# A tuned attention and feed-forward kernel: its program as a list of small steps in a searched order, with loads and stores on other queues and some transposes on TensorE

## Chip, cores and metric

One core of one Trainium2 chip. The metric is the device time of one execution in microseconds (us); lower is better. Single executions of one kernel agree within about 2%. Each time below is a median over runs, most of them "fast" (no run over 1.5% above the fastest of the same kernel); where slow runs matter, the text says so. "SyncE's queue" is the list of DMAs that SyncE issues, in order; "landing" is the time from the issue of a DMA until its data has arrived.

## The reference, cut to what matters

```python
def _attn_ref(q, k, v):                      # 8 batches, 8 heads, 576 tokens, 64 wide
    phi = lambda x: np.where(x > 0, x, np.exp(x) - 1.0) + 1.0
    q_p, k_p = phi(q), phi(k)
    kv = einsum('bhsd,bhse->bhde', k_p, v);  z = sum(k_p, axis=2)
    return einsum('bhsd,bhde->bhse', q_p, kv) / (einsum('bhsd,bhd->bhs', q_p, z)[..., None] + 1e-6)

x = attn.transpose(0, 2, 1, 3).reshape(4608, 512)
out = (((x @ w1) * (x @ w2)) @ w3) @ w_out   # d_ff 1024
```

All inputs and the output are float32 in HBM.

## The kernel before

Per batch it loads q, k and v (1 MB each plus small remainders for tokens 512 to 575), computes phi, forms kv on TensorE, transposes phi(q) into `qt` with a DMA transposition, multiplies (the "numerator units", tile `nd`), divides, and transposes the result `xn` into `xt` with another DMA transposition. The feed-forward part runs on chunks of 512 tokens: the gate (`a_ps`, `b_ps`, then `ab`) and the output (`o_ps`, with w3 and w_out folded into `wf` at the start). A hand-made order interleaves batch n + 1 with chunk n.

The parts that the change touches: who issues which DMA.

```python
def load_qkv(name, src, b, part=None):
    ...
    ins = nc.sync.dma_start(out=t[:, h0 * W:h1 * W]..., in_=src[b, h0:h1, 0:NJ * P, :]...)   # 1 MB
    if part != 1:
        for hh in range(2):                                                                  # remainders
            (nc.sync if part is None else nc.scalar).dma_start(out=t[hh * R:(hh + 1) * R, JW:]..., in_=...)

def qt_load(b, part):                       # part 0: qt, 512 KB; part 1: qtr, the remainder
    ...
    nc.sync.dma_start(out=dst, in_=src, transpose=True)

def xt_load(b, part):
    ...
    nc.sync.dma_start(out=dst, in_=src, transpose=True)

def o_unit(c, m):
    ...                                     # 8 matmuls, a copy to o_sb, then
    nc.gpsimd.dma_start(out=dst[:, j, :], in_=o_sb)
```

So loads and transpositions share SyncE's queue; GpSimd issues weights and stores. The order is text such as this, for the chunks from the fourth on (`L` load, `K`/`Q` phi, `KV`, `N` numerator unit, `X` xt, `T` qt, `V` copies of v, `F` gate, `O` output):

```python
NEXT = """KV F0 Lk Ke0 F1 Ks0 Ks1 O0 N0 Ke1 Ks2 Ks3 KsR F2 N1 O1 Lq N2 F3 N3 X0 Qe0 Qs0 Qs1
          O2 N4 X1 F4 Qe1 Qs2 O3 Lv F5 Qs3 QsR V T F6 F7"""
```

Of the kernel before, what the change touches and what calls it, by code (L numbers as in the profile page):

```python
# [13 lines left out]
P = 128  # L14
# [4 lines left out]
def kernel(  # L19
# [36 lines left out]
    ld = ctx.enter_context(tc.tile_pool(name="ld", bufs=5))  # L56
    setup = ctx.enter_context(tc.tile_pool(name="setup", bufs=2))
# [33 lines left out]
    def load_qkv(name, src, b, part=None):  # L91


        if part is None or part == 0:
            raw[name, b] = ld.tile([P, JW + RW], F32, tag="ld", name=f"{name}32")
        t = raw[name, b]
        h0, h1 = (0, H) if part is None else (4 * part, 4 * part + 4)
        W = NJ * D
        ins = nc.sync.dma_start(
            out=t[:, h0 * W:h1 * W].rearrange("p (h x) -> p h x", x=W),  # L100
            in_=src[b, h0:h1, 0:NJ * P, :].rearrange("h (p j) d -> p h (j d)", j=NJ))
        if part != 1:
            for hh in range(2):
                (nc.sync if part is None else nc.scalar).dma_start(
                    out=t[hh * R:(hh + 1) * R, JW:].rearrange("p (h d) -> p h d", d=D),
                    in_=src[b, hh * 4:(hh + 1) * 4, NJ * P:S, :].rearrange("h p d -> p h d"))
        return ins
# [4 lines left out]
    def phi_steps(name, b):  # L112
        x = raw[name, b]
        e = e_p.tile([P, JW + RW], BF16, tag="e", name="e")
        dj = phi_p.tile([P, KC, NJ, 2, D], BF16, tag=name + "j", name=name + "j")
        dr = phi_p.tile([P, RW], BF16, tag=name + "r", name=name + "r")
        ph[name, b] = (dj, dr)

        def ex(c0, c1):
            nc.scalar.activation(out=e[:, c0:c1], in_=x[:, c0:c1], func=AF.Exp)  # L120
            nc.vector.tensor_scalar_min(out=e[:, c0:c1], in0=e[:, c0:c1], scalar1=1.0)  # L121

        def st(out, ap):
            nc.vector.scalar_tensor_tensor(  # L124
                out=out, in0=ap(x), scalar=1.0, in1=ap(e), op0=ALU.add, op1=ALU.max)

        def pair(hp):
            for u in range(2):
                h = 2 * hp + u
                st(dj[:, hp, :, u, :], lambda t: t[:, h * NJ * D:(h + 1) * NJ * D].rearrange(  # L130
                    "p (j d) -> p j d", d=D))

        return dict(e0=lambda: ex(0, JW // 2), e1=lambda: ex(JW // 2, JW + (RW if b else 0)),
                    eR=lambda: None if b else ex(JW, JW + RW),
                    s0=lambda: pair(0), s1=lambda: pair(1), s2=lambda: pair(2),
                    s3=lambda: pair(3), sR=lambda: st(dr, lambda t: t[:, JW:]))

    def v_unit(b, parts=(0, 1, 2)):
        x = raw["v", b]
        for i in parts:  # L140
            if i < 2:
                nc.scalar.copy(  # L142
                    out=vt[:, :, 4 * i:4 * i + 4, 0:D],
                    in_=x[:, 0:JW].rearrange("p (h j d) -> p j h d", h=H, j=NJ)[
                        :, :, 4 * i:4 * i + 4])
            else:
                nc.scalar.copy(out=vr[:, :, 0:D], in_=x[:, JW:].rearrange("p (h d) -> p h d", d=D))
# [30 lines left out]


    def qt_load(b, part):  # L180
        qj, qr = ph["q", b]
        if part == 0:
            t = att.tile([P, KC, NJ * P], BF16, tag="qt", name="qt")
            src = qj.rearrange("p c j u d -> p (c j u d)")
            dst = t.rearrange("p c (j t) -> p (c j) t", t=P)
        else:
            t = att.tile([P, 2, P], BF16, tag="qtr", name="qtr")
            src, dst = qr, t
        qts[b, part] = t
        nc.sync.dma_start(out=dst, in_=src, transpose=True)  # L190

    def nat_unit(b, j):


        nd = at_ps.tile([P, 2, 512], F32, tag="at", name="nd")
        if j == 0:
            xns[b] = att.tile([P, NJ, H, D], BF16, tag="xn", name="xn")
        if j < NJ:
            n, dst = P, xns[b][:, j]
        else:  # L200
            n = R
            dst = xns[b, "R"] = att.tile([R, H, D], BF16, tag="xnr", name="xnr")
        for hp in range(KC):
            if j < NJ:
                w = qts[b, 0][:, hp, j * P:(j + 1) * P]
            else:
                hh, i = divmod(hp, 2)
                w = qts[b, 1][:, i, hh * R:(hh + 1) * R]
            for u in range(2):
                rows = slice(u * D, (u + 1) * D)  # L210
                nc.tensor.matmul(nd[0:n, u, hp * (D + 1):(hp + 1) * (D + 1)], w[rows],  # L211
                                 kvs[b][rows, hp, u, :], start=True, stop=True)
        v4 = nd[0:n, :, 0:KC * (D + 1)].rearrange("p u (c e) -> p u c e", e=D + 1)
        r = lr.tile([P, 2, KC], F32, tag="r", name="r")
        nc.vector.tensor_scalar_add(out=r[0:n], in0=v4[:, :, :, D], scalar1=1e-6)
        nc.vector.reciprocal(out=r[0:n], in_=r[0:n])
        nc.vector.tensor_tensor(  # L217
            out=dst.rearrange("p (c u) e -> p u c e", u=2), in0=v4[:, :, :, 0:D],
            in1=r[0:n].unsqueeze(3).to_broadcast([n, 2, KC, D]), op=ALU.mult)
# [15 lines left out]
    def first_tr(g):  # L235
# [4 lines left out]
        for i in range(2):  # L240
            for j in range(NJ):
                nc.tensor.transpose(tp[:, i * NJ + j, :],  # L242
                                    qj[:, 2 * g + i, j].rearrange("p u d -> p (u d)"), ident)
        nc.scalar.copy(out=qts[0, 0][:, 2 * g:2 * g + 2, :].rearrange("p i (j t) -> p (i j) t", t=P),
                       in_=tp)

    def first_kv(g):
        kv_half(0, g)
        for n in "zn":
            kvz[n, g] = att.tile([P, 2, 2, D], BF16, tag="kv" + n, name="kv" + n, bufs=2)  # L250
        t = kvs[0][:, 2 * g:2 * g + 2]
# [4 lines left out]
    def first_nd(hp, own):  # L256
# [6 lines left out]
        for i, n in ((1, "z"), (0, "n")):  # L263
            nc.tensor.matmul(nd[i], kvz[n, g][:, a].rearrange("p h e -> p (h e)"),
                             qts[0, 0][:, hp], start=True, stop=True)

        def finish():
            r = lr.tile([P, 512], F32, tag="lr", name="lr", bufs=2)
            nc.scalar.activation(out=r, in_=nd[1], func=AF.Ln, bias=eps[:, 0:1])
            nc.scalar.activation(out=r, in_=r, func=AF.Exp, scale=-1.0)  # L270
            nc.vector.tensor_tensor(
                out=xt[:, 0:NJ, hp, :], in0=nd[0].rearrange("p (j t) -> p j t", t=P),
                in1=r.rearrange("p (j t) -> p j t", t=P), op=ALU.mult)
        return finish
# [25 lines left out]
    def o_unit(c, m):  # L300
# [6 lines left out]
        nc.scalar.copy(out=o_sb, in_=o_ps)  # L307
        kind, b, j = order[c * (NCH // P) + m]
        if kind == "J":
            dst = out[b * S:b * S + NJ * P, :].rearrange("(p j) n -> p j n", j=NJ)  # L310
            nc.gpsimd.dma_start(out=dst[:, j, :], in_=o_sb)  # L311
        else:
            for i in range(2):
                nc.gpsimd.dma_start(
# [21 lines left out]
    def load_w3(i):  # L336
        if i % 4 == 0:
            t = ld.tile([P, JW + RW], F32, tag="ld", name="w3b")
            w3s[i // 4] = t[:, 0:JW].bitcast(BF16).rearrange("p (i n) -> p i n", i=4)
# [6 lines left out]
    def w3_tr(i):  # L346
# [4 lines left out]
        nc.scalar.copy(out=t, in_=tp)  # L351

    def wf_mm(i):
# [4 lines left out]
        nc.scalar.copy(out=wf_sb[:, i, :], in_=ps)  # L358


    def run(steps, names):
        for n in names.split():
            steps[n]()

    ctx.enter_context(tc.manual_schedule())
    src = {"k": k, "q": q, "v": v}

    def load(name, b, part=None):
        return load_qkv(name, src[name], b, part)

    first_loads = [load(n, 0, i) for i in range(2) for n in "kqv"]
    nc.scalar.preload_act_table_set("natural_log_exp_and_others")
    wl = [i for x in range(4) for i in load_w12(x)]
    after(wl[0], first_loads[3])
    wl += [load_wo(0), load_wo(1)]
    wl += [load_w3(i) for i in range(FC)]

    ks, qs = phi_steps("k", 0), phi_steps("q", 0)
    run(ks, "e0 s0 s1 eR sR")
    run(qs, "e0 s0 s1 eR sR")  # L380
    v_unit(0, (0, 2))
    run(ks, "e1 s2 s3")
    run(qs, "e1 s2 s3")
    first_tr(0)
    v_unit(0, (1,))
    first_kv(0)
    first_tr(1)
    fin = [first_nd(0, True), first_nd(1, True)]
    first_kv(1)
    for fn in fin:  # L390
        fn()
    fin = [first_nd(2, False), first_nd(3, False)]
    qt_load(0, 1)
    for fn in fin:
        fn()

    first = [f_open(0, 0), f_open(0, 1)]
    for n, kc in enumerate(range(KC)):
        for f in range(2):
            for ps, w in zip(first[f], (w1_sb, w2_sb)):  # L400
                nc.tensor.matmul(ps, w[:, kc, f * P:(f + 1) * P], xt[:, 0:4, kc, :],
                                 start=(n == 0), stop=(n == KC - 1))
    for f in range(2):
        f_close(0, f, *first[f])
    after(load("q", 1), wl[11])
    load("k", 1)
    load("v", 1)
    for f in range(2, FC):
        f_unit(0, f)
        if f >= 6:  # L410
            w3_tr(f - 6)




    def slots(text, c, a, n, load_b):
        ks = qs = None
        if n < B and n > 0:
            ks, qs = steps[n]
        for u in text.split():  # L420
            if u[0] == "F":
                f_unit(c, int(u[1]))
            elif u[0] == "O":
                o_unit(c - 1, int(u[1]))
            elif u[0] == "W":
# [83 lines left out]
```

## Time and profile before

| | before |
|---|---|
| median time | 278.87 us at first, 278.03 with the later run |
| profiled span | 276.8 us |
| TensorE, VectorE, ScalarE busy | 86%, 57%, 51% |
| mean granted TensorE clock | 0.983 |
| qt transposition, issue to landing (min, median, max) | 3.8, 7.2, 7.8 us |

The page of a profile has three parts that are used here: the busy time of each engine with its share of the span; a strip of 40 equal slices, in which each digit is the busy tenths of a slice (9 is 90% or more); and the DMA issues with their median time to landing. The timeline of one engine gives start, length and group, and in brackets the idle time just before and what ended it. The chain of waits goes back from the last instruction and says which work set the end. The prediction below shows the lines of each.

### The profile page before, as it was taken

What the parts mean: (1) busy time and instruction counts of PE and PEld (TensorE: products, weight loads), DVE (VectorE), ACT (ScalarE), POOL (GpSimd) and SP (SyncE); (2) the same over time, 40 slices, a digit from 0 to 9 for tenths busy, and PEclk for the clock granted to TensorE, in tenths of its full rate; (3) what the DMA queues carried; (4) which work ended last, traced back from release to release, by engine and by line L of the source; (5) the groups of instructions that cost most, each with busy time, mean ns of one, the idle gap of its engine ahead of it and who ended that gap; (6) DMA issues with size and microseconds to landing.
All of it is one profiled execution on the core that took longest, in us unless ns stands there. A gap on an engine that the chain in (4) does not pass through costs nothing.

```text
span 276.8 us, 4349 instructions
## 1 busy us (share of the span) xinstructions
PE 238.2 (86%) x1592; PEld 110.6 (40%) x1592; DVE 157.5 (57%) x382; ACT 139.9 (51%) x209; POOL 35.4 (13%) x70
## 2 busy tenths in 40 slices
PE   0268999987399586999899999999999999999980
PEld 0233455433144233444345444444544444444430
DVE  0855421756947985997795797698656332232200
ACT  1937467956525537375456548465623333333330
POOL 2473100002000000000200010021001002001021
PEclk9999999979979999999999999999999999999998
DMA  7999999987999699969999879826413402202122
GB/s 227 317 154 200 210 233 359 286 243 249 194 259 359 178 279 273 332 155 226 289 272 239 236 253 218 198 59 142 126 39 89 112 18 70 65 22 78 54 99 53
DMA packets 81189, 51.66 MB, mean 187 GB/s; under 512 B 48144, under 2 KB 77840, under 8 KB 81168
## 3 DMA queue, kind: packets, MB, share of 16 engines
q1 hardware_dynamic: 70160, 36.32, 50.8%
q0 software_dynamic: 9376, 14.68, 21.9%
q10 hardware_dynamic: 1632, 0.39, 0.6%
q8 instruction: 12, 0.20, 0.3%
q14 instruction: 9, 0.07, 0.1%
HBM read 38.80 MB, written 9.44 MB: 174 GB/s over the span
## 4 chain that ended last, share of the span: by engine, by line
PE 70%; DMA 13%; DVE 6%; ACT 5%; issue 2%; SPq 1%; ACTq 0%; POOL 0%; POOLq 0%; DVEq 0%
PE a_ps L285 21%; PE o_ps L304 20%; PE b_ps L285 19%; DMA qt<-qj 6%; ACT e L120 3%; PE nd L211 2%; PE kvp L170 2%; DMA xt<-xn 2%; DMA q<-in_q_dram 2%; PE wf_ps L356 2%; DMA v<-in_v_dram 2%; DMA k<-in_k_dram 2%; DVE kj L124 2%; DVE qj L124 1%; DVE e L121 1%
## 5 line engine op out<-in xcount | busy, mean ns | idle before, releaser
L291 DVE TENSOR_TENSOR ab<-a_sb,b_ps 128x512 bf16<-128x512 f32 x72 | 49.3, 685 | 64.2 <-PE b_ps L285 60.5
L285 PEld LDWEIGHTS <-w_sb 128*128 128x128 bf16 x560 | 53.1, 99 | 70.8 <-DMA xt<-xn 8.2
L285 PE MATMUL a_ps<-xt,w_sb 128*128 128x512 bf16 x280 | 73.0, 384 | 7.2 <-DMA xt<-xn 7.2
L285 PE MATMUL b_ps<-xt,w_sb 128*128 128x512 bf16 x280 | 72.7, 383 | 0.0
L304 PE MATMUL o_ps<-wf_sb,ab 128*128 128x512 bf16 x288 | 69.1, 386 | 0.0
L290 ACT COPY a_sb<-a_ps 128x512 f32<-128x512 f32 x72 | 42.1, 586 | 50.0 <-PE a_ps L285 48.7
L307 ACT COPY o_sb<-o_ps 128x512 f32<-128x512 f32 x36 | 21.1, 586 | 61.4 <-PE o_ps L304 61.4
L311 POOL DMA_DIRECT2D out_dram<-o_sb x32 | 17.5, 546 | 197.8 <-ACT o_sb L307 197.8
L304 PEld LDWEIGHTS <-ab 128*128 128x128 bf16 x288 | 27.4, 99 | 32.3 <-issue 1.6
L121 DVE TENSOR_SCALAR e<-e 128x1024 bf16<-128x1024 bf16 (+2 forms) x34 | 14.8, 436 | 19.9 <-ACT e L120 19.8
L124 DVE SCALAR_TENSOR_TENSOR qj<-q,e 128x256 bf16<-128x256 f32 x64 | 23.3, 419 | 0.5
L124 DVE SCALAR_TENSOR_TENSOR kj<-k,e 128x256 bf16<-128x256 f32 x64 | 23.0, 420 | 0.4
L217 DVE TENSOR_TENSOR xn<-nd,r 128x512 bf16<-128x512 f32 x28 | 19.4, 691 | 1.0
L120 ACT ACTIVATE e<-k 128x1024 bf16<-128x1024 f32 (+2 forms) x17 | 18.8, 1114 | 0.0
L120 ACT ACTIVATE e<-q 128x1024 bf16<-128x1024 f32 (+2 forms) x17 | 18.6, 1107 | 0.0
L142 ACT CAST vt<-v 128x1024 bf16<-128x1024 f32 x16 | 16.1, 1058 | 0.0
L356 PE MATMUL wf_ps<-wo_sb,w3t 128*128 128x512 bf16 x64 | 14.8, 379 | 0.0
L242 PE MATMUL tp<-ident,qj 128*128 128x128 bf16 x16 | 2.4, 308 | 13.6 <-DVE qj L124 13.5
L175 DVE TENSOR_TENSOR kv<-kvf,kvp 128x260 bf16<-128x260 f32 x16 | 6.7, 424 | 8.7 <-ACT kvf L174 8.5
L170 PE MATMUL kvp<-vt,kj 64*128 64x130 bf16 x256 | 11.2, 228 | 0.5 <-ACT vt L142 0.3
L170 PEld LDWEIGHTS <-kj 64*128 64x128 bf16 x256 | 8.9, 99 | 5.5 <-issue 4.9
L211 PE MATMUL nd<-kv,qt 64*128 64x65 bf16 x224 | 8.0, 193 | 3.1 <-DMA qt<-qj 3.0
(52 smaller groups left out, 128.9 us busy)
## 6 DMA issues: line engine op xcount, KB each, us to landing
out_dram<-o_sb POOLq DMA_DIRECT2D x32, 256.0 KB, 3.5
q<-in_q_dram SPq DMA_DIRECT2D x7, 1024.0 KB, 8.2
k<-in_k_dram SPq DMA_DIRECT2D x7, 1024.0 KB, 6.4
v<-in_v_dram SPq DMA_DIRECT2D x7, 1024.0 KB, 6.9
w_sb<-in_moe_w_dram POOLq DMA_DIRECT2D x8, 256.0 KB, 8.4
w3b<-in_moe_w_dram POOLq DMA_DIRECT2D x8, 256.0 KB, 12.5
k<-in_k_dram SPq DMA_DIRECT2D x2, 512.0 KB, 4.8
q<-in_q_dram SPq DMA_DIRECT2D x2, 512.0 KB, 5.2
```

Source lines behind the costliest of these rows:

```text
L120: nc.scalar.activation(out=e[:, c0:c1], in_=x[:, c0:c1], func=AF.Exp)
L121: nc.vector.tensor_scalar_min(out=e[:, c0:c1], in0=e[:, c0:c1], scalar1=1.0)
L124: nc.vector.scalar_tensor_tensor(out=out, in0=ap(x), scalar=1.0, in1=ap(e), op0=ALU.add, op1=ALU.max)
L170: nc.tensor.matmul(kvp[:, r, i * W:(i + 1) * W], kk[rows], vv[rows], start=(n == 0), stop=(n == (NJ if r == g else NJ - 1)))
L217: nc.vector.tensor_tensor(out=dst.rearrange("p (c u) e -> p u c e", u=2), in0=v4[:, :, :, 0:D], in1=r[0:n].unsqueeze(3).to_broadcast([n, 2 ...
L285: nc.tensor.matmul(ps, w[:, kc, f * P:(f + 1) * P], xt[:, 4 * c:4 * c + 4, kc, :], start=(kc == 0), stop=(kc == KC - 1))
L290: nc.scalar.copy(out=a_sb, in_=a_ps)
L291: nc.vector.tensor_mul(out=abs_[c][:, f, :], in0=a_sb, in1=b_ps)
L304: nc.tensor.matmul(o_ps, ab[:, f, m * P:(m + 1) * P], wf_sb[:, f, :], start=(f == 0), stop=(f == FC - 1))
L307: nc.scalar.copy(out=o_sb, in_=o_ps)
L311: nc.gpsimd.dma_start(out=dst[:, j, :], in_=o_sb)
L356: nc.tensor.matmul(ps, w3ts[i][:, kc, :], wo_sb[:, kc, :], start=(kc == 0), stop=(kc == FC - 1))
```

## The change

The intent: TensorE should no longer starve between 55 and 112 us. The program becomes 485 small steps in an order that a search on an event model found. Loads no longer stand in one in-order queue with transpositions: GpSimd issues those of q, k and v from the second batch on, SyncE the transpositions and the stores. Beside that, batches 1 and 2 get `xt` from TensorE transposes, some copies move from ScalarE to VectorE, and the first batch's remainder is done like its main part. The core of the diff:

```diff
-        ins = nc.sync.dma_start(
+        return (nc.gpsimd if b else nc.sync).dma_start(
             out=t[:, h0 * W:h1 * W].rearrange("p (h x) -> p h x", x=W),
...
+                (nc.sync if alt else nc.gpsimd).dma_start(          # remainders, own tiles
...
+    def xt_tr(b, j, alt=False):
+        tp = mm_ps.tile([P, NCH], F32, tag="mm", name="xtp")...
+        for kc in range(KC):
+            nc.tensor.transpose(tp[:, kc, :], x[:, kc * P:(kc + 1) * P], ident)
+        copy_of(alt)(out=xt[:, tile_of["J", b, j]], in_=tp)
...
-            nc.gpsimd.dma_start(out=dst[:, j, :], in_=o_sb)
+            nc.sync.dma_start(out=dst[:, j, :], in_=o_sb)
...
+    ORDER = """
+    N0.0 N0.3+ L0.3+ L0.0 x0.0 L0.1 B0 y0.0 M0.0 x0.2 x0.1 C0 y0.2 M0.1 z0.0 v0.2+ X0.0 y0.1 E0
...
+    Z1.2 W4+ W5+ F0.6 w6 X1.2 y1.0 z1.0 Z1.3 T1.0 z1.1 F0.7 x1.2 y1.2 N1.0 N1.1 L2.3+ z1.4 M2.2
+    z1.2 w7 v1.2 v1.0 W6+ W7 z1.3 Y1.2 L2.2 v1.1 K1.0+ O0.0+ K1.1+ X2.0 Z1.4 O0.1 A1.0 x2.2 M0.3
...
+    for s in ORDER.split():
+        step(s)
```

In the list `L`, `M`, `N` are the loads of k, q, v (part 2 is the 1 MB, part 3 the remainder), `T` is a qt transposition (part 0 the large one, part 1 qtr), `D` an xt transposition, `P` its form on TensorE, `A` numerator units, `F` and `O` gate and output; a plus moves a copy to VectorE, or a remainder load to SyncE (behind `K`, the kv product, it means the form used before).

## The prediction

> **What bounds the kernel now.** I read the page first, then the chain of waits, then the timeline of TensorE alone, then the waits of SyncE's queue.
>
> The page's busy shares and its strip of 40 slices (6.92 us each):
>
> ```profile
> PE 238.2 (86%) x1592; PEld 110.6 (40%) x1592; DVE 157.5 (57%) x382; ACT 139.9 (51%) x209; POOL 35.4 (13%) x70
> ...
> PE   0268999987399586999899999999999999999980
> ...
> DVE  0855421756947985997795797698656332232200
> ...
> PEclk9999999979979999999999999999999999999998
> DMA  7999999987999699969999879826413402202122
> ```
>
> From the 17th slice (111 us) to 269 us TensorE works at 90% or more in all slices but one. It is hungry only before: a ramp, then low slices around 55 to 112 us. The DMA engines are near full until about 165 us, but not after it. So the second half is bound by TensorE and the middle by what feeds it. The timeline of TensorE shows the holes (start, length, instruction group, in brackets the idle time before it and what ended it):
>
> ```profile
> 57.69 0.21 PE L170 MATMUL kvp<-vr,kr 64*128 64x130 bf16 x1 [0.85 <-ACT vr L147]
> ...
> 59.04 3.51 PE L304 MATMUL o_ps<-wf_sb,ab 128*128 128x512 bf16 x8
> ...
> 62.86 1.90 PE L304 MATMUL o_ps<-wf_sb,ab 128*128 128x512 bf16 x8
> ...
> 68.78 0.31 PE L211 MATMUL nd<-kv,qtr 64*64 64x65 bf16 x8 [1.58 <-DVE r L215]
> ...
> 75.38 1.10 PE L285 MATMUL a_ps<-xt,w_sb 128*128 128x512 bf16 x4 [4.46 <-DMA xt<-xn]
> ...
> 91.59 0.31 PE L211 MATMUL nd<-kv,qtr 64*64 64x65 bf16 x8 [1.73 <-DVE xn L217]
> ...
> 98.18 1.04 PE L285 MATMUL a_ps<-xt,w_sb 128*128 128x512 bf16 x4 [2.71 <-DMA xt<-xn]
> ...
> 110.74 0.30 PE L211 MATMUL nd<-kv,qt 64*128 64x65 bf16 x8 [1.53 <-DMA qt<-qj]
> ...
> 132.58 0.30 PE L211 MATMUL nd<-kv,qt 64*128 64x65 bf16 x8 [1.45 <-DMA qt<-qj]
> ```
>
> Each hole ends with a transposed tile (xt, qt) or a VectorE result. With three smaller ones (0.30, 0.17, 0.81) they sum to 15.6 us. One group of eight o_ps matmuls spans 3.51 us after such a pause, the next 1.90: the pause also costs clock. The chain of waits says why transposes are late: loads, transposes and their waits share SyncE's queue.
>
> ```profile
> 82.73 2.04 SPq L104
> 84.81 4.38 DMA v<-in_v_dram
> ...
> 96.86 5.47 DMA q<-in_q_dram
> 102.88 7.81 DMA qt<-qj
> ```
>
> And the waits of SyncE's own queue (who waited for what: us in total, times, longest):
>
> ```profile
> SPq L229 <- DVE xnr L217: 24.0, 2, 15.0
> SPq L99 <- DMA w3b<-in_moe_w_dram: 20.0, 1, 20.0
> ...
> SPq L229 <- DVE qj L124: 15.1, 3, 12.0
> ```
>
> While a transpose (L229) waits there for VectorE, no load behind it can start.
>
> **The floor under it.** In full-clock stretches four 512-column matmuls follow each other in 0.86 us on the chain, so one costs 0.216. After the first gate matmul (on the chain at 23.9 us) TensorE still owes: 576 a/b x 0.216 = 124.4; 288 o_ps x 0.216 = 62.2; 64 wf x 0.216 = 13.8; 64 w3 transposes x 0.056 (16 took 0.90) = 3.6; kv of seven batches x 1.12 = 7.8; 36 numerator units x 0.24 (start to start) = 8.6. Sum 220.4. So 23.9 + 220.4 = 244.3 would be its end. It ends at 269.2: 24.9 us are lost. Of these 15.6 are the holes; about 4.5 are clock (1.7 in the slow o_ps group, 1.9 in the three slow groups after 75.4, 0.9 at the start); the remaining 4.8 are pauses of about 0.1 before units that change weights. The tail from 269.2 to 276.8 is 7.6: copy, store, landing.
>
> **What the Trainium skill says.** "DMA: Bandwidth & Descriptors", section "Issuing engines are not separate DMA queues": all issuing engines feed the same 16 DMA engines, a second issuer saves only issue time. So moving loads to GpSimd gives no bandwidth; its value here must be order. The trace agrees that order is the trouble (the 12 and 15 us waits above) and can't show the other. "SBUF — State Buffer", section "SBUF: two separate sides", the "DVE blocks DMA" trap: GpSimd can't write descriptors while VectorE runs an operation in a 2-port mode. The minima (L121) and some new copies may be such; at 0.42 us each, 34 of them, I expect little. No row of before tests it: its GpSimd issues took 0.53 to 0.81 us, and nothing hung on them. "TensorE: Matmul & The Clock Gate", Part 1: an idle window of about 3.4 us halves the clock. The trace agrees: 3.51 against 1.90 us, and a granted mean of 0.83 from 70 to 80 us.
>
> **The change part by part.**
> (1) Loads leave SyncE. Per batch its queue now issues three loads with six remainder loads, roughly 0.55 + 1.3 to 2.8 each, some 8 us, in front of or behind transposes. In the new program only the first batch and six later remainder pairs stay there. GpSimd takes 1 MB loads of 1,024 pieces; its 512-piece weight load took 0.81 and a 128-piece one 0.53, so about 1.2 us each is an estimate from these, some 2 to 3.5 a batch with remainders, on an engine busy 13%. Stores move to SyncE at about 0.5 each, 4 to 5 a chunk, behind transposes that take 1.2 to 5.2 us to issue: this can hold a store, and its four buffers tolerate some delay.
> (2) Batch 1 and 2 get xt by TensorE: 32 transposes x 0.056 in 8 units, with weight changes about 0.25 a unit, +2.0 us on the bound engine, and 8 copies of about 0.6 off it. They take a 5.1 us landing (the xt row) plus a wait of a queue out of the way of the first two chunks. The 4.46 hole at 75.4 becomes VectorE's chain for two units, 2 x (0.16 + 0.20 + 0.69) = 2.1, plus a copy 0.6, half under an o_ps unit of 1.73: I allow 1.5.
> (3) Twenty-nine copies go to VectorE (12 of o_sb, 7 wf, 2 w3t, 6 of v, 1 qt, 1 xt). With about 0.65 us mean that is near 20 us off ScalarE's 139.9 and on VectorE's 157.5. VectorE would be at some 67% of a 265 us span: not the bound.
> (4) The first batch's kv skips the partial sum (copy 0.38, addition 0.42, twice), but v's first parts are loaded ahead of k and two v copies enter VectorE early (about 1.4 us). VectorE ran almost without pause from 8.1 to 17.7 there, so I leave the start of the gate at 23.9, give or take 1.5.
> (5) Numerator units of one batch are issued in pairs (21 calls for 35 units): some weight pauses go. The first batch's remainder (r) costs the same.
> (6) Order: the second load of q no longer waits 20 us for w3, and steps are spread to keep TensorE fed. From the list I see kv, o_ps and gate units put between each transposition and its reader. Still it is tight: the qt transposition of batch 2 has about 9.8 us of TensorE work ahead of its reader and needs about 9.5 (VectorE 1.05, queue 1.2, landing 7.2). I expect residual holes of 3.5 in all besides the 1.5.
>
> Sum: start 23.9 + demand 220.4 + added transposes 2.0 + holes 5.0 + clock 2.5 + small pauses 4.0 + tail 7.0 (the store's issue beside it may be shorter) = 264.8 of span. The profiled run took 278.56 for a span of 276.8, so 1.8 more: about **266.5 us**, 4.4% less.
>
> **The rivals.** A: *the order is modelled, the chip differs.* A fixed order on in-order queues turns each mis-sized duration into a wait. For it: qt landings spread from 3.8 to 7.8 us, and transposes take 1.6 to 5.2 us to issue. Half the holes would return: 272 to 274. B: *DMA is the bound.* For it: DMA shares of 0.85 to 1.35 up to 180 us. If GpSimd's queue moved loads 10% slower, the first four batches come late and 5 to 8 us return: about 273. Against: before had the third batch's k, q and v in by 90 us, well ahead of where even a shifted schedule (about 98) wants them. C: *SyncE becomes the jam*, stores behind transposes that wait for VectorE: with o_sb held, TensorE stalls after the fourth store; 268 to 280. Against: only 0.5 us per store and some 20 us of chunk time. D: *the search succeeds fully*: holes 1, clock 1, pauses 3, start 1 earlier: 258 to 259.
>
> **Range and chances.** D sets the low end, A and B the high end: 258.5 to 274. Faster by over 2% means under 273.3, which A or B alone about reaches and C passes: chance 0.84; within 2% 0.12; slower 0.04.
>
> **What would show it.** TensorE's strip at 9 from the fifth slice on with at most three lower digits; idle before a_ps behind xt under 2 us; 85 to 88% as share stays near or rises to 89%, as about 238 minus little busy time lies in a shorter span; granted clock at 1.0 in 60 to 80; first gate matmul near 24 us; VectorE about 175, ScalarE about 120 us. I am wrong if the gate starts later than 26, if PE waits for q, k, v loads, or if o_sb copies wait for stores.

## The result, and the profile after

The changed kernel takes 311.86 us (median of 4 runs, 309.03 to 322.26; the 322.26 is a slow run) against 278.03. The ratio is 1.120, with a 95% interval of 1.107 to 1.133: 12% slower. A ratio here is the mean time of one kernel's fast runs over that of the other's fast runs of the same rounds, so not quite the ratio of the medians.

The page of the changed kernel, its busy shares and its strip (now 7.68 us a slice):

```profile
PE 241.6 (79%) x1594; PEld 114.0 (37%) x1608; DVE 168.2 (55%) x421; ACT 128.0 (42%) x202; POOL 54.5 (18%) x86
...
PE   0099999878960898009995992799979999999994
...
DVE  0684359566950787006973871487678573434320
...
PEclk9999999997996799657997998799999999999998
DMA  6999998997199739971899399934916405200113
```

Between 54 and 84 us (slices 8 to 11) TensorE stays at 7 to 9 tenths, where it fell to 3 before. Then slice 13 (92 to 100 us) and slices 17 and 18 (123 to 138 us) are empty, on VectorE too. The DMA engines are busy there (9, 9 and 7 tenths). The timeline of TensorE names what ends the holes:

```profile
69.96 1.70 PE L358 MATMUL a_ps<-xt,w_sb 128*128 128x512 bf16 x4 [1.08 <-ACT xt L273]
...
100.64 0.62 PE L252 MATMUL nd<-kv,qt 64*128 64x65 bf16 x16 [11.15 <-DMA qt<-qj]
...
101.19 3.42 PE L377 MATMUL o_ps<-wf_sb,ab 128*128 128x512 bf16 x8
...
138.34 0.62 PE L252 MATMUL nd<-kv,qt 64*128 64x65 bf16 x16 [16.66 <-DMA qt<-qj]
...
164.81 0.42 PE L252 MATMUL nd<-kv,qt 64*128 64x65 bf16 x16 [3.26 <-DMA qt<-qj]
...
193.61 0.62 PE L252 MATMUL nd<-kv,qt 64*128 64x65 bf16 x16 [7.63 <-DMA qt<-qj]
...
224.33 0.42 PE L252 MATMUL nd<-kv,qt 64*128 64x65 bf16 x16 [1.99 <-DMA qt<-qj]
```

The 4.46 us hole before the second chunk is down to two waits, 1.65 (68.5 us, for a copy of the TensorE transposes) and 1.08. But qt, which ended holes of 1.5 us before, now ends holes of 11 and 17. The chain of waits of the changed kernel shows the transpositions themselves (start, length):

```profile
82.58 18.01 DMA qt<-qj
...
113.25 25.04 DMA qt<-qj
...
151.85 12.90 DMA qt<-qj
...
176.58 16.98 DMA qt<-qj
...
214.52 9.77 DMA qt<-qj
```

The large holes come from landings of 13 to 25 us; all seven are 9.4, 18.0, 25.0, 12.9, 17.0, 9.8 and 3.7 us. 27% of the chain is DMA of qt, against 5.6% before. The waits of SyncE's own queue have changed as well (L283 issues xt, L384 the stores; us in total, times, longest):

```profile
SPq L283 <- DVE ab L364: 41.5, 3, 23.0
SPq L384 <- ACT o_sb L380: 37.9, 13, 14.7
```

No load stands behind such a wait any more. A transposition can, behind a store that waits for its copy. The DMA issues (destination, source, queue, count, size, median us to landing), the kernel before:

```profile
q<-in_q_dram SPq DMA_DIRECT2D x7, 1024.0 KB, 8.2
...
qt<-qj SPq DMA_TRANSPOSE x7, 7.2
```

and after:

```profile
q<-in_q_dram POOLq DMA_DIRECT2D x7, 1024.0 KB, 12.8
...
qt<-qj SPq DMA_TRANSPOSE x7, 12.9
```

Nearly the same bytes (50.6 MB for 51.7) on the same 16 DMA engines: q loads take 1.6 times as long, k loads 12.3 us for 6.4, v loads only 7.8 for 6.9, transpositions 1.8 times. From 113.2 to 138.3 us the engines were busy (share 1.01) at 149 GB/s; the four other long landings had 157, 341, 201 and 188 GB/s. Before the change five stretches around a transposition ran at 187 to 287 GB/s.

### The profile page after: what moved, and what is told of

It reads as the page before. It is cut to its first block, busy times and chain, and to the rows that moved or that the text cites. A ratio compares the mean times of both kernels' runs of the same rounds, so it can differ in the third digit from the quotient of the medians.

```text
span 307.3 us, 4395 instructions
## 1 busy us (share of the span) xinstructions
PE 241.6 (79%) x1594; PEld 114.0 (37%) x1608; DVE 168.2 (55%) x421; ACT 128.0 (42%) x202; POOL 54.5 (18%) x86
## 4 chain that ended last, share of the span: by engine, by line
PE 56%; DMA 33%; DVE 4%; ACT 3%; SPq 2%; issue 2%; ACTq 0%; DVEq 0%
DMA qt<-qj 27%; PE o_ps L377 17%; PE a_ps L358 16%; PE b_ps L358 15%; DMA k32r<-in_k_dram 3%; DMA q<-in_q_dram 2%; PE wf_ps L429 2%; PE nd L252 2%; DVE qj L149 1%; SPq L98 1%; PE w3p L423 1%; ACT lr L322 1%; ACT e L124 1%; PE kvp L206 1%; PE kvp L186 1%
## 5 line engine op out<-in xcount | busy, mean ns | idle before, releaser
L358 PE MATMUL a_ps<-xt,w_sb 128*128 128x512 bf16 x288 | 78.6, 394 | 1.3 <-ACT xt L273 1.1
L358 PE MATMUL b_ps<-xt,w_sb 128*128 128x512 bf16 x288 | 77.6, 390 | 0.4 <-DVE xt L326 0.4
L377 PEld LDWEIGHTS <-ab 128*128 128x128 bf16 x288 | 27.6, 99 | 32.8 <-issue 1.6
L252 PE MATMUL nd<-kv,qt 64*128 64x65 bf16 x224 | 6.5, 202 | 41.8 <-DMA qt<-qj 41.8
L380 ACT COPY o_sb<-o_ps 128x512 f32<-128x512 f32 x24 | 13.9, 585 | 38.4 <-PE o_ps L377 38.3
L258 DVE TENSOR_SCALAR r<-nd 128x8 f32<-128x8 f32 (+1 forms) x35 | 4.9, 160 | 42.8 <-PE nd L252 42.6
L107 POOL DMA_DIRECT2D v<-in_v_dram x8 | 7.0, 878 | 103.6 <-ACT vt L158 52.3
L128 DVE TENSOR_SCALAR e<-e 128x1024 bf16<-128x1024 bf16 x32 | 13.4, 426 | 18.2 <-ACT e L124 18.2
L252 PEld LDWEIGHTS <-qt 64*128 64x128 bf16 x224 | 4.7, 101 | 47.9 <-DMA qt<-qj 44.4
L124 ACT ACTIVATE e<-k 128x1024 bf16<-128x1024 f32 x16 | 16.8, 1058 | 7.5 <-DMA k<-in_k_dram 7.4
L124 ACT ACTIVATE e<-q 128x1024 bf16<-128x1024 f32 x16 | 16.8, 1058 | 2.0 <-DMA q<-in_q_dram 2.0
L380 DVE COPY o_sb<-o_ps 128x512 f32<-128x512 f32 x12 | 8.3, 689 | 14.5 <-PE o_ps L377 14.3
## 6 DMA issues: line engine op xcount, KB each, us to landing
q<-in_q_dram POOLq DMA_DIRECT2D x7, 1024.0 KB, 12.8
k<-in_k_dram POOLq DMA_DIRECT2D x7, 1024.0 KB, 12.3
w_sb<-in_moe_w_dram POOLq DMA_DIRECT2D x8, 256.0 KB, 11.6
w3b<-in_moe_w_dram POOLq DMA_DIRECT2D x8, 256.0 KB, 11.8
```

What stands on the lines that cost most here:

```text
L124: nc.scalar.activation(out=e, in_=x, func=AF.Exp)
L128: nc.vector.tensor_scalar_min(out=e, in0=e, scalar1=1.0)
L252: nc.tensor.matmul(nd[0:n, u, hp * (D + 1):(hp + 1) * (D + 1)], w[rows], kvs[b][rows, hp, u, :], start=True, stop=True)
L358: nc.tensor.matmul(ps, w[:, kc, f * P:(f + 1) * P], xt[:, 4 * c:4 * c + 4, kc, :], start=(kc == 0), stop=(kc == KC - 1))
L377: nc.tensor.matmul(o_ps, ab[:, f, m * P:(m + 1) * P], wf_sb[:, f, :], start=(f == 0), stop=(f == FC - 1))
L380: copy_of(alt)(out=o_sb, in_=o_ps)
```

## The experiments

Two theories at first. **Ring theory:** a transposition beside loads of another queue has to share the DMA engines with them and comes out badly; in the kernel before, both stood in one queue, so a transposition ran ahead of all loads issued after it. **Order theory:** the new list simply asks for qt too early, and the engines are as good as before. Two more for parts of the change: **jam** (stores on SyncE hold the transpositions) and **remainders** (the small loads of 256-byte pieces do the harm).

### One part of the change alone

`e1_order_only`: the new list, the old queues.

```diff
-        return (nc.gpsimd if b else nc.sync).dma_start(
+        return nc.sync.dma_start(
-                (nc.sync if alt else nc.gpsimd).dma_start(
+                nc.sync.dma_start(
-            nc.sync.dma_start(out=dst[:, j, :], in_=o_sb)
+            nc.gpsimd.dma_start(out=dst[:, j, :], in_=o_sb)
```

> The new list of steps, but all loads of q, k, v on SyncE's queue and the stores on GpSimd's, as before the change. Ring theory: the landing of the qt transposition falls from 12.9 to about 7 us (a FIFO again), TensorE's waits for qt from 42 to under 10 us, and the time to about 270, at or under the kernel before. Order theory: the waits stay, over 300 us.

Measured: 287.94 us, ratio 1.033 (1.027 to 1.040). qt lands in 5.2 us at the median (12.0 at most), and TensorE's waits for it are 1.6 us in all: the transposition is cured, as the ring theory says. The time is better than the change but not under the kernel before, so that half of the expectation missed: on these queues the list has other holes, 3.89 us for first weights (`w_sb`), 3.85 for `vt` and 7.14 behind a VectorE result.

`e3_queues_only`: the old order, the new queues.

```diff
-        ins = nc.sync.dma_start(
+        ins = (nc.gpsimd if b else nc.sync).dma_start(
-                (nc.sync if part is None else nc.scalar).dma_start(
+                (nc.gpsimd if part is None else nc.scalar).dma_start(
-            nc.gpsimd.dma_start(out=dst[:, j, :], in_=o_sb)
+            nc.sync.dma_start(out=dst[:, j, :], in_=o_sb)
```

> The old order of the kernel before, with the loads from the second batch on issued by GpSimd and the stores by SyncE. Ring theory: qt landing of 12 us or more, waits for qt on TensorE of 20 us or more, time 290 to 310. Order theory: qt lands in about 7 us and the time stays within 3% of before.

Measured: 324.88 us median, but three of the four runs (and the profiled one) count as slow; the single fast run took 314.05, some 13% over before, so there is no ratio with an interval. In the profiled run qt lands in 7.3 us at the median and 28.7 at most, and TensorE's matmuls wait 55 us for it. The queues alone do about the whole damage. The seven landings tell when: three transpositions that went out 0.2 to 1.1 us behind a 1 MB load of k or v took 28.7, 22.7 and 25.4 us; two that went out 0.8 us ahead of one took 7.2 and 7.3; two that met no load took 3.9 and 3.8. So the median stayed low.

`e6_stores_pool`: the change, with only the stores put back on GpSimd.

```diff
-            nc.sync.dma_start(out=dst[:, j, :], in_=o_sb)
+            nc.gpsimd.dma_start(out=dst[:, j, :], in_=o_sb)
```

> The changed kernel with only the stores put back on GpSimd's queue. Ring theory: qt still lands in 12 us or more, 300 to 320 us. Jam theory (stores on SyncE hold the transpositions): qt lands in about 7 us, under 285 us. Stores behind blocked loads on GpSimd's queue may add waits for o_sb buffers.

Measured: 302.24 us, ratio 1.087 (1.079 to 1.094). A qt transposition still takes up to 24.7 us and one still ends a hole of 16.35. The median landing, 8.8, was lower than expected (the profiled run is a slow one). The jam theory is out as the main cause; the stores' place is worth some 9 us (fast runs of two different rounds).

`e10_rem_sp`: the change, with only the remainder loads moved to SyncE.

```diff
-                (nc.sync if alt else nc.gpsimd).dma_start(
+                nc.sync.dma_start(
```

> The changed kernel with only the small remainder loads (64 KB, pieces of 256 B) moved from GpSimd to SyncE's queue; the 1 MB loads stay on GpSimd. If the remainder pairs are what makes the transpositions so slow in the kernel, qt lands in 10 us or less and the time falls to 280 to 292. If the 1 MB loads do it, qt still takes 12 us or more in the middle and the time stays at 300 to 315.

Measured: 307.47 us, fast runs 301.67 and 304.97 (two of four are slow). qt lands in 12.9 us at the median and 18.9 at most, and the holes are 10.42, 10.53, 3.49 and 8.29. The 1 MB loads are enough for the trouble. The worst case is 18.9 us here and 25.0 with the remainders on GpSimd, one profile each; `m4_late` below has more on that.

### The transposition by itself

Four kernels of DMAs only. Their result is wrong (zeros); what counts is the landing of one 512 KB transposition from SyncE, three times in each company.

> A kernel of DMAs only (its result is wrong on purpose: zeros). One transposition of 512 KB from SyncE, alone and beside two 1 MB loads issued from GpSimd, from ScalarE, or ahead of it on SyncE's own queue; also with loads cut in pieces of 256 B and 8 KB; each three times, in phases. Ring theory (transposition and loads on different queues share the engines badly): alone about 4 us, 14 us or more beside GpSimd's loads, and loads of 12 us or more where they alone take 7; on SyncE's own queue about 10 in all (loads 7, then 4). If only GpSimd's descriptors matter, ScalarE's loads leave the transposition at 10 or less; if any second queue does it, they slow it as well. If packets take turns, pieces of 8 KB slow it more and pieces of 256 B less. Order theory (the list asks too early, the DMA engines are as good as before): no phase over 10 us.

In `m1_rings` the transposition took 4.3 us alone, 8.7 beside two GpSimd loads, 10.4 beside two ScalarE loads, and 9.4 behind two loads on its own queue. Pieces of 8 KB in place of 1 KB changed nothing (8.4 from GpSimd, 10.7 from ScalarE). The expected 14 us or more were missed. This run was built badly: the transposition was issued ahead of the loads and had a lead. Its 512 KB are 2,080 packets (the units in which the DMA engines move data); with 8 KB pieces 1,987 of them had moved by 218 us, beside 27 of the loads, and with 256-byte pieces all 2,080, beside 9. So it could not decide, and says nothing on the size of pieces.

> DMAs only again (zeros as result). The first such kernel gave a transposition beside two loads only 8.7 us, about what the loads needed, so it may simply finish when they do. Here it starts when a first load has landed and 0, 1, 2 or 4 more loads of 1 MB from GpSimd are under way or queued; also 4 from ScalarE, 4 behind it on SyncE's own queue, 4 pairs of remainder loads (64 KB each, pieces of 256 B), and a mix of 2 loads and 3 pairs. Starved-transposition theory: 4 us with none, growing with every load, 14 us or more with four, from ScalarE too; 5 or less with the four behind it on its own queue. If the remainder pairs are what hurts: their phase and the mix are over 10 us, four plain loads under 8.

In `m2_overlap` it starts when a first load has landed, with 0, 1, 2 or 4 more loads under way (with 1: 4.7 us). The DMA issues:

```profile
Tnone<-qj SPq DMA_TRANSPOSE x3, 4.3
...
Tpooltwo<-qj SPq DMA_TRANSPOSE x3, 7.6
Tpoolfour<-qj SPq DMA_TRANSPOSE x3, 13.7
Tactfour<-qj SPq DMA_TRANSPOSE x3, 12.6
Tspfour<-qj SPq DMA_TRANSPOSE x3, 4.3
```

Four loads on another queue make it 13.7 us from GpSimd or 12.6 from ScalarE, and four loads behind it on its own queue leave it at 4.3. The four of another queue were asked for just ahead of it; in `m1_rings` the two of another queue came just after it, and it still cost 8.7. That is the ring theory without any kernel around it. (Four remainder pairs alone: 4.4; two loads and three pairs: 9.5.)

The packet counts say how the loads hold it up. In the first such stretch, 119.9 to 134 us (queue of GpSimd's loads, then SyncE's with the transposition: packets, MB, share of the engines):

```profile
q0 software_dynamic: 993, 3.81, 78.9%
q1 hardware_dynamic: 2080, 0.52, 20.2%
```

A packet has about 4 KB on GpSimd's queue and 0.25 KB in the transposition. From 126 to 128 us the loads moved 160 packets (0.66 MB) and the transposition also 160 (0.04 MB); from 128 to 130 us 176 and 177. Three quarters of the transposition moved after 131 us, when the loads were nearly done; it landed 1.2 us after the last of them. ScalarE's loads have packets of 1.0 KB: from 190 to 192 us 572 of theirs (0.58 MB) went beside 572 of the transposition's (0.15 MB). So beside plain loads the two queues take turns, one packet each, and the queue with the small packets gets few bytes. The Trainium skill, "DMA: Bandwidth & Descriptors", section "Queues, rings and completion order", says that each DMA engine goes round the queues that have work, one packet at a time; these counts agree.

> DMAs only (zeros as result). In the changed kernel one qt transposition took 25.0 us beside three loads of 1 MB and three remainder pairs from GpSimd, with a small transposition behind it; in the last kernel of DMAs four loads cost 13.7 and a mix of two loads and three pairs 9.5. Here the same company as in the 25 us case: three loads and three pairs, with and without the small transposition, three loads alone, six pairs alone, the mix with two stores ahead, and the mix from ScalarE. If it is the company alone, the mix takes 20 us or more and one of the parts shows which member does it. If it is not, all phases stay under 14, and the rest comes from the kernel around it.

`m3_mix` gave the transposition the company of the 25 us case, three loads and three remainder pairs. With the transposition issued first: 8.8 to 9.8 at the median (three plain loads 7.8 to 8.1, six pairs 5.7, the mix from ScalarE 11.6). With two stores ahead of it, so that it came in just behind the first load: 26.4 us. That reproduced the kernel's number, and left open whether the stores or the later start did it. One stretch without stores hints at the start: in the very first the load happened to go out 0.55 us ahead of the transposition, and that took 20.1.

> DMAs only (zeros as result). The transposition again beside three loads and three remainder pairs from GpSimd, now with two stores ahead of it on SyncE's queue, or with a small transposition ahead instead; with stores ahead and three or six plain loads, six pairs only, one load; the mix from ScalarE; and all on SyncE's own queue behind it. If stores do it: 20 us or more with stores, 10 with the small one ahead. If the late start does it: 20 or more with both. If the remainder pairs in the mix do it: three plain loads 8 to 11 and six plain 16 to 20, the mix over 20. On its own queue 5 to 6 us whatever follows.

`m4_late` tells these apart. The transposition behind two stores, beside three loads and three pairs from GpSimd (`Tstores`), three and six plain loads, the mix from ScalarE, and the mix behind it on its own queue:

```profile
Tstores<-qj SPq DMA_TRANSPOSE x3, 27.6
...
Tnorem<-qj SPq DMA_TRANSPOSE x3, 14.3
Tnoremsix<-qj SPq DMA_TRANSPOSE x3, 23.2
...
Tactlate<-qj SPq DMA_TRANSPOSE x3, 12.8
Townqueue<-qj SPq DMA_TRANSPOSE x3, 4.8
```

With a small transposition ahead in place of the stores it took 19.7, so the late start matters more than the stores. Behind two stores, one load costs 8.7, three 14.3, six 23.2, and six remainder pairs without a 1 MB load 8.2. The first stretch of `Tstores` and of `Tnorem` (its bounds and length, then busy time of VectorE and GpSimd, clock, DMA share, GB/s):

```profile
61.30:89.00 27.70, 0.00 (x0) 5.96 (x9) 1.00 0.90 165
...
215.00:229.20 14.20, 0.00 (x0) 2.20 (x3) 1.00 1.00 293
```

These show two effects. Beside plain loads no bandwidth is lost (293 GB/s): the transposition is merely last. With remainder pairs in the mix the engines move 165 GB/s at nearly the same busy share (0.90 against 1.00), which is like what the kernel showed in its 25 us wait (149). From ScalarE the mix took 12.8, but that is no clean comparison: its queue was held on the way, and its third load was issued only when the transposition had all but landed.

Equal turns explain the first effect: beside six plain loads the counts are again 162 and 162 packets (274 to 276 us). Why the mix from GpSimd nearly halves the rate stays open. There the counts differ (169 packets of the loads and 449 of SyncE's from 67 to 70 us), and no run took the mix apart further.

### Taking the overlap away in the kernel

`e4_turns`: the change as it is, with 1 MB loads and large qt transpositions taking turns.

```diff
+        if b and turn.get("T") is not None:
+            after(ins, turn["T"])            # a load waits for the transposition ahead of it in the list
+        if b:
+            turn["L"] = ins
...
-        nc.sync.dma_start(out=dst, in_=src, transpose=True)
+        ins = nc.sync.dma_start(out=dst, in_=src, transpose=True)
+        if part == 0:
+            if turn.get("L") is not None:
+                after(ins, turn["L"])        # and the transposition for the last load ahead of it
+            turn["T"] = ins
```

> The changed kernel with one addition: each qt transposition waits until the last 1 MB load ahead of it in the list has landed, and each 1 MB load behind it waits until the transposition has landed. The queues stay as in the change. Ring theory: qt lands in about 4 to 5 us once issued, chain share of qt small, time 262 to 280. Order theory: the added waits only cost, over 310 us.

Measured: 272.32 us, ratio 0.981 (0.976 to 0.986): added waits bring the changed kernel from 12% behind the kernel before to 2% ahead of it (the interval excludes "no change" but not 2%, so a verdict at 2% is unclear). Its DMA issues and its largest remaining hole:

```profile
qt<-qj SPq DMA_TRANSPOSE x7, 3.8
```

```profile
61.65 0.62 PE L192 MATMUL kvp<-vt,kj 64*128 64x130 bf16 x8 [6.38 <-ACT vt L164]
```

This is the run that settles the main cause: nothing was changed but when 1 MB loads and large transpositions may overlap. The order theory foretold over 310.

`e5_qt_pe`: the change, with the seven large transpositions done by TensorE.

```diff
+            for g in range(2):
+                tp = at_ps.tile([P, 8, P], BF16, tag="at", name="tpq")
+                for i in range(2):
+                    for j in range(NJ):
+                        nc.tensor.transpose(tp[:, i * NJ + j, :], qj[:, 2 * g + i, j]..., ident)
+                copy_of(g)(out=t[:, 2 * g:2 * g + 2, :]..., in_=tp)
+            return
```

> The changed kernel with the seven large qt transpositions done by TensorE (16 transposes of 128x128 and two copies each), all loads still on GpSimd. Ring theory: the long waits for qt vanish; seven times 16 x 0.056 = 6 us more on TensorE, some new waits for PSUM and copies as the list was not made for it; xt transpositions still share engines with loads: 268 to 285 us. Order theory: over 300 us.

Measured: 274.43 us, ratio 0.988 (0.982 to 0.993): 1% under the kernel before. So the loss also goes away by a second way, one without added waits. Its new holes are small ones around the transposes (1.65, 1.28 and 1.69 the largest after 100 us).

`e12_before_turns`: the old order on the new queues, with the same turns.

> The old order with loads on GpSimd and stores on SyncE (324.9 us without turns), now with turns between qt transpositions and 1 MB loads. Ring theory: qt lands in about 4 us again and the time returns to 270 to 285. If it stays over 300 us, the old order on these queues is bad for another reason. The difference to the changed kernel with turns (272.3) is the worth of the new list of steps.

Measured: 292.82 us, ratio 1.041 (1.033 to 1.050), outside what was expected. qt lands in 3.8 us, so the turns work; but here all seven batches use DMA transpositions for xt as well, these have no turns, and one of them ended the largest hole:

```profile
109.78 1.89 PE L292 MATMUL a_ps<-xt,w_sb 128*128 128x512 bf16 x4 [16.09 <-DMA xt<-xn]
```

That transposition was issued at 92.0 us, with loads of q and v from GpSimd around it, and landed after 17.7 us; the median of xt before the change was 4.4. So the same harm came through the other door, and this run can't price the list against the old order. That price stays open.

### A version that beats both

`e7_turns_v` is the kernel with turns, plus one edit to the list: the two halves of batch 1's v load stand ahead of its qt transposition.

```diff
-    Z1.2 W4+ W5+ F0.6 w6 X1.2 y1.0 z1.0 Z1.3 T1.0 z1.1 F0.7 x1.2 y1.2 N1.0 N1.1 L2.3+ z1.4 M2.2
+    Z1.2 W4+ W5+ F0.6 w6 X1.2 y1.0 z1.0 Z1.3 N1.0 N1.1 T1.0 z1.1 F0.7 x1.2 y1.2 L2.3+ z1.4 M2.2
```

> The kernel with turns, with one more edit: the loads of v for the second batch stand ahead of the first qt transposition in the list, so they need not wait for it. It should take away the 6.4 us hole before the second batch's kv at 61 us and nothing else: 265 to 269 us, 3 to 5% under the kernel before. If the hole only moves to the wait for qt, 270 to 273.

Measured: 270.93 us, ratio 0.974 (0.968 to 0.980). The 6.38 us hole is gone, but 4.55 us came back in a wait for qtr at 79 us, so the gain is smaller than expected (and at 2% the verdict is unclear).

`e8_turns_vt` also moves batch 1's qtr transposition ahead of three stores (`T1.1` from behind `F1.0` to behind `Z1.4`).

> The last version with turns and one more move: the small transposition (qtr) of the second batch stands where its input is ready, ahead of three stores, not behind them. The 4.55 us wait for qtr at 79 us should go: 266 to 269 us, 3.5 to 4.5% under the kernel before. If the wait only moves on, 270 to 272.

Measured: 269.09 us, ratio 0.967 (0.961 to 0.973). The wait moved again, to the next qtr, of the first batch (3.97 at 82 us): about the old size. The fast runs have a median of 269.02, a hair outside 266 to 269, and the gain of 3.3% is just short of the 3.5 foretold.

`e9_loads_wait` drops one half of the turns: the transposition no longer waits for loads ahead of it.

```diff
-            if turn.get("L") is not None:
-                after(ins, turn["L"])
```

> As the run before it, but one half of the turns only: loads behind a qt transposition wait for it, while the transposition no longer waits for the loads ahead. Loads ahead then share the engines with it, so qt lands in 5 to 12 us instead of 3.8, but is issued earlier by as much: within 1.5% of the other, 264 to 272 us. If loads ahead starve it as those behind do, 275 or more.

Measured: 269.68 us, but three of six runs count as slow; the fast ones took 265.95 to 268.67, ratio 0.961 (0.953 to 0.970), the same as the run before within the intervals. qt lands in 4.2 us at the median, 9.7 at most. So it is enough to hold back the loads that come after.

`e11_all_turns` lets loads wait for qtr too (`turn["T"] = ins` for both parts).

> The version in which loads behind a qt transposition wait for it, now for the small qtr transpositions as well. If the small ones suffer from loads as the large do, the wait of 4.6 us for qtr at 82 us goes and the time is 264 to 268 us; if the added waits hold back loads, 270 or more.

Measured: 268.36 us (265.44 to 269.00), ratio 0.957 (0.952 to 0.962): the best of these versions, though its interval overlaps that of the one before. It is 4.3% under the kernel before. The qtr hole fell from 4.59 to 2.68 us.

## Why the prediction was wrong

It said 266.5 us, within 258.5 to 274.0; the changed kernel takes 311.86. Its own sum (start of the gate, demand on TensorE, added transposes, holes, clock and pauses, tail) can be filled in from the trace after:

| term | predicted | in the trace after |
|---|---|---|
| first gate matmul | 23.9 | 23.2 |
| demand and added transposes | 220.4 + 2.0 | 222.4, taken over |
| holes on TensorE | 5.0 | 45.3, the brackets of its timeline summed |
| clock and small pauses | 2.5 + 4.0 | 11.8, what is left |
| tail | 7.0 | 4.6 |
| span | 264.8 | 307.3 |

The step that failed is in part (6), "needs about 9.5 (VectorE 1.05, queue 1.2, landing 7.2)", together with "residual holes of 3.5 in all". It carried the 7.2 us landing of the kernel before into a program where loads no longer queue behind the transposition. The landing was a property of the shared queue. It became 12.9 at the median and 25.0 at most; for batch 2 itself it was 18.0, 10.8 more than allowed, and its reader waited 11.15. Of the 45.3 us of holes 41.8 are matmuls that wait for qt (1.10, 11.15, 16.66, 3.26, 7.63 and 1.99). The clock term followed: after the long holes TensorE restarts slowly, 3.42 us for an o_ps group at a granted clock of 0.53 (100.6 to 104.5 us), as against 1.89 later on.

Point by point:

- **Part (1), loads leave SyncE.** The issue cost was right: GpSimd needs 0.9 us a 1 MB load (estimate 1.2). (Five later remainder pairs stay on SyncE, not six.) The sentence "moving loads to GpSimd gives no bandwidth; its value here must be order" was half an argument. It took order as only to gain. The kernel before had a priority in its queue order, and the change gave it away.
- **Part (2), xt by TensorE.** Right in direction: the hole before the second chunk went from 4.46 to 2.73 (1.65 + 1.08 at its two waits), but 1.5 was allowed.
- **Part (3), copies.** Direction right, size too large: VectorE 168.2 us (about 175 foretold), ScalarE 128.0 (about 120).
- **Part (4), the start.** Right within its margin, 23.2 for 23.9.
- **Part (6), order.** The first half is borne out: from the start of the gate to 66 us TensorE has no pause over 1.10. The clock was not: "granted clock at 1.0 in 60 to 80" came true for 60 to 70 us (0.87 before, 1.00 after), but from 70 to 80 it is 0.83 as before, with TensorE busy all the time.
- **Rival B** was the nearest, but as written ("moved loads 10% slower", about 273) it looked at the loads as the victims and at 5 to 8 us. The runs show transpositions as the victims, 12.9 us for 7.2 at the median and 25.0 for 7.8 at most, and q loads at 12.8 for 8.2. **Rival C**, the jam of stores, is worth some 9 us and was refuted as the cause by the run with the stores put back. **Rival A** named the mechanism of amplification rightly: one mis-sized duration in a fixed order becomes a wait on every queue. **Rival D** (258 to 259) was reached by no run; the fastest single one with the overlap taken away took 265.4.
- **Two readings of the trace before.** "Each hole ends with a transposed tile or a VectorE result" is not quite so: those of 0.30, 0.85 and 0.81 end with a ScalarE copy (vt, vr). And the slow o_ps group (3.51 us, granted clock 0.53) does not follow an idle stretch of 3.4 us: the three pauses ahead of it add up to 1.3 us. The 4.46 us hole, with 0.50 granted from 77 to 79 us, fits the passage cited better.
- What was to show it wrong ("if PE waits for q, k, v loads, or if o_sb copies wait for stores") named neither qt nor its landing, though the best sum in the text stood on that number with 0.3 us to spare.

With turns, the same list runs in 272.3 us; with two small moves in it as well, in 268.4 to 269.7. Both are inside the predicted range, so the sum was near for a program in which the landing holds.

## What to carry to other kernels

When a load and a latency-critical DMA share a queue, the queue is also a priority: what is issued first goes first (a transposition took 4.3 us with four loads behind it and 9.4 behind two). On two queues they took turns by packets, and the one with small packets was last. Before moving loads to another issuer, ask which short transfer on the critical path ran undisturbed only because the loads stood behind it, and take its duration from a stretch where it has company. If it must have its own queue, let the loads that come after it wait for its landing: here such waits took the changed kernel from 12% over the kernel before to 2% under it, and to 3 to 4% with two moves in the list.

## What the Trainium skill lacked or had wrong

- "DMA: Bandwidth & Descriptors", section "Issuing engines are not separate DMA queues" (and the row on spreading DMAs in "Rules for kernel authors"): it says that another issuer only saves issue time. It can also cost: a 512 KB transposition took 4.3 us with four 1 MB loads behind it on its own queue, 13.7 and 12.6 with four just ahead of it on GpSimd's or ScalarE's.
- The same page, "Rules for kernel authors": "A transpose next to ordinary DMAs needs nothing". All kernels here that were meant to be right stayed so, but in time it needs something: beside one, three and six loads of another queue (and behind two stores) it took 8.7, 14.3 and 23.2 us.
- No page says what turns by packets mean for a transposition: 160 of its packets carried 0.04 MB while 160 of a load's carried 0.66.
- No page has what a mix does: three 1 MB loads and three pairs of small loads in 256-byte pieces from GpSimd stretched it to 27.6 us at 165 GB/s in all, three 1 MB loads alone to 14.3 us at 293 GB/s.
- The pages give rates of a DMA transposition, but none the time from issue to landing of one within SBUF: 4.3 us for [128, 2048] bf16 alone in the kernel of DMAs, 3.8 in the kernel with turns.
- "SBUF — State Buffer", the "DVE blocks DMA" trap, is neither confirmed nor contradicted: in `m4_late` VectorE did nothing (0.00 us) while a transposition took 27.6, and GpSimd's issues took 0.9 us each in the changed kernel, so it is not needed for what was seen.
